# Decode layer on one core: VectorE's instructions for two groups as a loop of seven turns, with semaphores counted down

## The chip, the cores and the metric

One core of one Trainium2 chip runs the whole kernel. The metric is the device time of one execution in microseconds; the kernel before has a median of 1291.82 us in three runs (1291.61 to 1292.01).

## The reference

One decode step of a transformer layer, batch 4, one query position, model width 512: layer norm, attention with 32 heads of 128 over a cache of 8192 positions for each head, output projection, residual, a second layer norm, a gated feed-forward block of width 1792, residual. All tensors are bfloat16.

```python
q = (layernorm(x) @ wq).reshape(B, 1, 32, 128).transpose(0, 2, 1, 3)
scores = einsum("bhqd,bhkd->bhqk", q, k_cache) * 128 ** -0.5
o = einsum("bhqk,bhkd->bhqd", softmax(scores), v_cache)
h = x + o.transpose(0, 2, 1, 3).reshape(B, 1, 4096) @ wo
n = layernorm(h)
out = h + (sigmoid(n @ w_gate) * (n @ w_up)) @ w_down
```

The two caches have 268 MB each; the weights add about 14 MB.

## The kernel before

**Pairs and groups.** The 128 (batch, head) combinations are taken two at a time: 64 pairs (`NP`), each with 4 MB of K and 4 MB of V. Four pairs (`GP`) make a group, and a group's softmax is done at once; there are 16 groups. The steps (L365) are K of pairs 0 to 3, and then K of pair n + 4 and V of pair n in turn (`LAGP` is 4). Each step has eight chunks (`NCH`).

**Transfers.** SyncE (SP) issues every large load in the order of the list of steps, into the four slots of `KV` (L327 to L335). A slot is taken again when its last user is done: `freed` (L312) gives the token of the last `scores` of a K pair or of the last `pv` of a V pair, and SP's queue waits for it ahead of the DMA. The feed-forward weights use the same slots at the end; `w_down` comes in three pieces (`WDT`, L342). K of pair 0 and V of pair 63 come in four pieces each. `wo` is loaded over `wq` once the q projection (`t_qproj`) has been computed (L360).

**A K step.** For each chunk VectorE transposes 128x1024 words out of `KV` into one of four buffers `kTc` (`transposes`, L410 to L413), and TensorE multiplies them with the masked query windows `Lq` (`scores`, L430). VectorE fills the four `Lq` buffers ahead (`q_windows`, L574 to L578). After a group's fourth pair `softmax` (L441) takes maximum, exponential, sum and division through VectorE, TensorE and ScalarE, in four parts p1 to p4 that are due 1, 3, 6 and 8 chunks later; p4 writes the probabilities, transposed, into `PT` (L484).

**A V step.** `pv` (L487) multiplies `PT` with V on TensorE. After a group's last pair, `finish` (L514) evicts the sum with ScalarE, collects rows (L523) and, for each second group, makes `O_row` and `OT` on VectorE (L528, L530), projects with `wo` (L540) and adds to `sth` (L545).

**Order and semaphores.** `_Prog` collects a list of instructions for each engine. `emit` (L76) works out which semaphores an instruction has to wait for, and `_wait` (L70) puts the wait ahead of it. VectorE and ScalarE have two semaphores each: one for what TensorE waits for (`dve>pe`, `act>pe`), one for all others. TensorE has one, `pe`, that only goes up. What TensorE waits for is counted down again by the waiter (`sem_inc(..., -v)`, L74), so that each wait is for the same number in each turn of a loop.

**The loop.** TensorE's list is cut (L592 to L599) ahead of K of pairs 8, 16, ..., 56 and of V of pair 60. The seven stretches between are equal and are run as one body in `Fori`, seven turns (L698 to L710). The lists of the other engines, VectorE's among them (L692), are written out in full.

**After the loop** come the last four V steps, the residual and second layer norm (`layernorm`, L238), the feed-forward block (L635 to L642), `f_res` (L651), the three parts of `f_down` (L659 to L663), the eviction to `o_sb` (L668) and the store (L669).

Of the kernel before, what the change touches and what calls it, by code (L numbers as in the profile page):

```python
# [5 lines left out]
BF16 = mybir.dt.bfloat16  # L6
# [5 lines left out]
NSL = 4  # L12
NKT = 4
# [7 lines left out]
class _Prog:  # L21
# [6 lines left out]

    ENGS = ("sp", "act", "dve", "pool", "pe")
    SPLIT = ("dve", "act")  # L30
# [14 lines left out]
    def _as_seen(self, eng, t):  # L45
        key, v = t
        if key not in self.SPLIT:
            return t
        want = (eng == "pe")
        for to_pe, n in self.kind[key][v - 1:]:  # L50
            if to_pe == want:
                return (key + ">pe" if want else key + ">", n)
# [23 lines left out]
    def emit(self, eng, fn, waits=(), incs=1, to_pe=False, sig=None):  # L76
# [4 lines left out]
        if eng in self.SPLIT and incs:  # L81
            assert incs == 1
# [14 lines left out]
        if eng == "pe":  # L97
            run.same = (sig, tuple(todo), incs)
        return tok

    def dma(self, eng, key, fn, waits=()):
# [8 lines left out]
        return tok  # L110


def bass_sequential_preLN__mha_block_cached__glu_gated_glu__decode_kernel(
# [32 lines left out]
    with ExitStack() as es:  # L146
# [19 lines left out]
        q2 = SB("q2", [128, 4, NH], BF16)  # L166
# [45 lines left out]
        keys = ["sp", "act>", "act>pe", "dve>", "dve>pe", "pool", "pe", "x", "out", "wg", "wu", "wd0", "wd1", "wd2", "wq", "wo"]  # L212
        prog.own = {f"vs{i}" for i in range(NSL)}
# [24 lines left out]
        def layernorm(st, t_st, i, dst, mbank, t_bank):  # L238
            w = lnw[:, i, :]
            n = NDC * B  # L240
            t1 = emit("dve", lambda e: e.tensor_tensor(st[:, n:2 * n], st[:, 0:n], st[:, 0:n], ALU.mult), [t_st])

            tr = emit("dve", lambda e: e.tensor_reduce(
                lnr[:, i, :], st[:, :].rearrange("p (k c) -> p k c", c=NDC), AX.X, ALU.add), [t1], to_pe=True)
            t2 = emit("pe", lambda e: e.matmul(mbank[:, 0:2 * B], onesf[:, :], lnr[:, i, :], start=True, stop=True),
                      [tr, t_ones, t_bank])
            t3 = emit("dve", lambda e: e.tensor_copy(w[:, 0:2 * B], mbank[:, 0:2 * B]), [t2])
            t4 = emit("dve", lambda e: e.tensor_tensor(w[:, 8:8 + B], w[:, 0:B], w[:, 0:B], ALU.mult), [t3])
            t5 = emit("dve", lambda e: e.scalar_tensor_tensor(
                out=w[:, 12:12 + B], in0=w[:, B:2 * B], scalar=EPS, in1=w[:, 8:8 + B],  # L250
                op0=ALU.add, op1=ALU.subtract), [t4])
            ts = emit("act", lambda e: e.activation(w[:, 20:20 + B], w[:, 12:12 + B], ACT.Sqrt), [t5])
# [4 lines left out]
                cen, st[:, 0:n].rearrange("p (b c) -> p b c", b=B), mean, ALU.subtract), [t3])  # L257
            t6 = emit("dve", lambda e: e.reciprocal(w[:, 16:16 + B], w[:, 20:20 + B]), [ts])
            return emit("dve", lambda e: e.tensor_tensor(
                dst[:, :].rearrange("p (b c) -> p b c", b=B), cen, rstd, ALU.mult), [t6, t7], to_pe=True), t3  # L260
# [11 lines left out]
        t_xT = emit("pe", f_xT, [t_x, t_ident])  # L272
# [14 lines left out]
        for hh in range(2):  # L287
# [4 lines left out]
            amask[:, :], identf[:, :].rearrange("p (a j) -> p a j", a=4), AX.X, ALU.max), [t_identf])  # L292
# [8 lines left out]
        t_pv = {}  # L301
        t_wq = []
# [9 lines left out]
        def freed(job):  # L312
# [3 lines left out]
            t = t_score.get(NCH * n + NCH - 1) if kind == "k" else t_pv.get(n)  # L316
# [93 lines left out]
        def transposes(n, s):  # L410
# [3 lines left out]
                kTc[:, u % NKT, :], chunk(n, slot, s)), [t_k[n][s * len(t_k[n]) // NCH], t_score.get(u - NKT)], to_pe=True)  # L414
# [24 lines left out]
        turn = {}  # L439

        def softmax(g):  # L441

            t_mx = emit("dve", lambda e: e.tensor_reduce(mpart[:, :], sbank(g), AX.X, ALU.max),  # L443
                        [t_score[GP * NCH * (g + 1) - 1], st_.get("p1")], to_pe=True)
            box = {}

            def p1():
                box["p1"] = emit("pe", lambda e: e.matmul(  # L448
                    bank[XS][0:1, 0:128], mpart[:, 0:1], identf[:, :], start=True, stop=True),
                    [t_mx, t_identf, st_["xs"]], sig="p1")  # L450
# [4 lines left out]
                    [box["p1"]])  # L455
                box["d2"] = emit("dve", lambda e: e.tensor_copy(
                    rowpad[0:1, :].rearrange("p (z k i) -> p z k i", z=2, i=GP),
                    bass.AP(raw(mrow), 0, [[GH, 1], [GP, 2], [0, 16], [1, GP]])), [d2, t_rp0], to_pe=True)

            def p2():  # L460
                t = emit("pe", lambda e: e.matmul(  # L461
                    bank[XS][:, 128:129], rowpad[:, :], identf[:, 0:1], start=True, stop=True),
                    [box["d2"], t_rp0], sig="p2")
                a1 = emit("dve", lambda e: e.tensor_scalar(  # L464
                    negmb[:, :], bank[XS][:, 128:129], -SCALE, None, op0=ALU.mult), [t])
                box["a2"] = emit("act", lambda e: e.activation(  # L466
                    E_sb[:, :], sbank(g), ACT.Exp, bias=negmb[:, 0:1], scale=SCALE, accum_out=sig[:, 0:1]),
                    [a1], to_pe=True)
                st_["exp"] = t_exp[g] = box["a2"]

            def p3():
                t = emit("pe", lambda e: e.matmul(  # L472
                    bank[XS][:, 130:131], Gmat[:, :], sig[:, 0:1], start=True, stop=True), [box["a2"], t_gm], sig="p3")
                d3 = st_["xs"] = emit("dve", lambda e: e.reciprocal(rsum[:, :], bank[XS][:, 130:131]), [t])  # L474
                box["d4"] = emit("dve", lambda e: e.tensor_scalar(
                    E_sb[:, :], E_sb[:, :], rsum[:, 0:1], None, op0=ALU.mult), [d3])

            def p4():
                pb = g % 2
                w = [box["d4"], t_pt0, t_pvg.get(g - 2)]  # L480
                for z in range(2):
                    dst = bass.AP(raw(PT), 64 * z * 2 * PTW + pb * PTW + 4 * z,
                                  [[2 * PTW, 64], [128, 2 * RC], [1, 4], [40, GP]])
                    t_ptc[g] = emit("dve", lambda e, z=z, dst=dst: e.transpose(dst, E_sb[64 * z:64 * z + 64, :]), w, to_pe=z == 1)  # L484
            return [(1, p1), (3, p2), (6, p3), (8, p4)]

        def pv(u):  # L487
# [20 lines left out]
            tok = emit("pe", f, w, incs=4 if last else 1, sig=("pv", slot, g % 2, i, m, n == 0, first, last))  # L508
# [5 lines left out]
        def finish(g):  # L514
            t_oev[g] = emit("act", lambda e: e.activation(O_sb[:, :], obank(g), ACT.Copy),  # L515
                            [t_pvg[g], st_.get("sel")], to_pe=True)
            lo = 64 * (g % 2)

            def s1():
# [6 lines left out]
                st_["sel"] = emit("pe", f, [t_oev[g], t_pk, st_["xo"]], sig=("collect", lo))  # L526
                if g % 2:
                    t = emit("dve", lambda e: e.tensor_copy(O_row[:, :], bank[XO][:, 0:128]),  # L528
                             [st_["sel"], st_.get("tr")])
                    st_["tr"] = emit("dve", lambda e: e.transpose(  # L530
                        OT[:, :, :], O_row[:, :].rearrange("p (i e) -> p e i", e=4)), [t, st_.get("ot")], to_pe=True)
                    st_["xo"] = t

            def s2():
                def f(e):
                    ins = None
                    for c in range(NDC):
                        for k in range(4):
                            at = (4 * turn.get("g", g // 2) + k) * D + 128 * c
# [4 lines left out]
                st_["ot"] = t = emit("pe", f, [st_["tr"], st_["xo"]], sig="project")  # L544
                st_["h"] = st_["xo"] = emit("dve", lambda e: e.tensor_tensor(  # L545
                    sth[:, 0:NDC * B], sth[:, 0:NDC * B], bank[XO][:, 128:128 + NDC * B], ALU.add), [t, st_["h"]])
            return [(2, s1), (4, s2)] if g % 2 else [(2, s1)]

        def q_projection():
# [8 lines left out]
            t = emit("pe", f, [t_wq[0], t_xn, t_xTc, t_h])  # L558
            t_qproj.append(t)
            tq = emit("dve", lambda e: e.tensor_copy(q_all[:, :], bank[XO][:, 0:NH]), [t], to_pe=True)  # L560

            def f2(e):
                ins = None
                for ce in range(4):
                    ins = e.matmul(bank[XO][:, NH * ce:NH * (ce + 1)], selrep[:, ce, :], q_all[:, :],
                                   start=True, stop=True)
                return ins
            t2 = emit("pe", f2, [tq, t_sr])
            st_["q"] = st_["xo"] = emit("dve", lambda e: e.tensor_copy(
                q2[:, :, :].rearrange("p e n -> p (e n)"), bank[XO][:, 0:4 * NH]), [t2])  # L570
# [3 lines left out]
        def q_windows(n):  # L574
            dst = bass.AP(raw(Lq), n % NLQ * 4 * W + 31, [[NLQ * 4 * W, 128], [W, 4], [64, 2], [32, 2]])
            src = bass.AP(raw(q2), GH * (n % NP // GP) + n % GP, [[4 * NH, 128], [NH, 4], [GP, 2], [0, 2]])
            keep = bass.AP(raw(amask), 0, [[4, 128], [0, 4], [2, 2], [1, 2]])
            t_lq[n] = emit("dve", lambda e: e.tensor_tensor(dst, src, keep, ALU.mult),  # L578
                           [st_["q"], t_lq0, t_am, t_score.get(NCH * (n - NLQ + 1) - 1)], to_pe=True)
# [13 lines left out]
        for kind, n in steps:  # L593
            if kind == "k" and n and n % (2 * GP) == 0:
                if not cuts:
                    emit("pe", lambda e: [], t_wo, incs=0)
                cuts.append(len(prog.ops["pe"]))
            if (kind, n) == ("v", NP - LAGP):
                cuts.append(len(prog.ops["pe"]))  # L599
            for m in range(NCH):  # L600
                u = NCH * n + m
                if kind == "k":
# [13 lines left out]
        while chain:  # L616
# [6 lines left out]
        emit("act", lambda e: e.activation(dummy[:, 0:1], sig[:, 0:1], ACT.Sqrt), [st_["xs"]])  # L623
        t_res = emit("dve", lambda e: e.tensor_copy(
            res[:, :, 0:25:8], sth[:, 0:NDC * B].rearrange("p (b c) -> p c b", b=B)), [st_["h"], t_rs0], to_pe=True)
# [4 lines left out]
        def glu_mm(wv, bk):  # L630
# [8 lines left out]
        t_g = emit("pe", glu_mm(t_w["wg"][0], bank[XO]), [t_hn, t_w["wg"][1], st_["xo"]])  # L639
        t_sg = emit("act", lambda e: e.activation(sg_sb[:, :], bank[XO][:, 0:NF], ACT.Sigmoid), [t_g])  # L640
        t_u = emit("pe", glu_mm(t_w["wu"][0], bank[UBK]), [t_hn, t_w["wu"][1]])
        t_hh = emit("dve", lambda e: e.tensor_tensor(  # L642
            hhT[:, :, 0:25:8], sg_sb[:, :].rearrange("p (t b) -> p t b", b=B),
            bank[UBK][:, 0:NF].rearrange("p (t b) -> p t b", b=B), ALU.mult), [t_sg, t_u, t_hh0], to_pe=True)
# [12 lines left out]
        t_r = emit("pe", f_res, [t_res])  # L657
        for i in range(len(WDT) - 1):
# [8 lines left out]
            t_d = emit("pe", f_down, [t_hh, t_wd[i], t_r], incs=4)  # L667
        t_oc = emit("dve", lambda e: e.tensor_copy(o_sb[:, :], bank[DBK][:, 0:128]), [t_d])  # L668
# [6 lines left out]
        with nc.Block() as block:  # L675
# [16 lines left out]
            def _(dve):  # L692
                for fn in prog.ops["dve"]:
                    fn(dve)

            @block.tensor
            def _(pe):
                ops = prog.ops["pe"]  # L698
                body = ops[cuts[0]:cuts[1]]
                for a, b in zip(cuts[1:], cuts[2:]):  # L700
                    assert [x.same for x in ops[a:b]] == [x.same for x in body]
                for fn in ops[:cuts[0]]:
                    fn(pe)
                with pe.Fori(0, len(cuts) - 1) as i:
                    turn["g"] = i
                    for fn in body:
                        fn(pe)
                    del turn["g"]
# [30 lines left out]
```

## Time and profile before

| what | before |
|---|---|
| median of three runs | 1291.82 us |
| the profiled execution, its own time | 1291.74 us |
| span in its profile, first to last instruction | 1290.0 us |
| bytes read from HBM | 550.77 MB, 427 GB/s over the span |
| TensorE matmul busy | 781.4 us (61%) |
| VectorE busy | 723.8 us (56%), 765 instructions |
| ScalarE, GpSimd busy | 28.0 us, 10.9 us |
| granted TensorE clock, mean | 0.792 |

The times in a page count from the first instruction. A group of instructions is a line with its engine, operation, tiles and number, then busy time and the mean of one, then the engine's idle time ahead of them with what ended it. "PEq L74" as the releaser is TensorE's own queue at the countdown of line 74.

Besides the instructions the trace keeps DMA packets, with queue, start and size, and the events by which a transfer counts its semaphore up: sixteen for each of the large loads, one by each DMA engine. Which engine an event belongs to isn't recorded. The table gives, for some loads, the time of the first of the sixteen events, and by how much the last and the second last of the sixteen came after it.

| load, first event at (us) | last event later by | second last later by |
|---|---|---|
| 17.48 | 0.38 | 0.38 |
| 42.40 | 1.53 | 0.37 |
| 52.13 | 1.52 | 1.23 |
| 236.68 | 1.94 | 1.92 |
| 246.39 | 2.22 | 1.94 |
| 294.96 | 2.24 | 1.93 |
| 314.38 | 3.06 | 2.25 |
| 460.10 | 3.04 | 2.25 |
| 469.82 | 3.24 | 3.04 |
| 683.52 | 3.27 | 3.03 |
| 703.07 | 4.12 | 2.91 |
| 897.36 | 4.13 | 2.88 |
| 916.80 | 5.11 | 2.88 |
| 1120.78 | 5.13 | 2.86 |
| 1140.20 | 6.10 | 2.87 |
| 1247.06 | 6.13 | 2.86 |
| 1256.76 | 6.20 | 3.28 |
| 1282.02 (last piece of `w_down`) | 4.89 | 2.02 |

Packets of the kind "instruction" are in two queues. Queue 8 has twelve of 16,384 bytes, at 18.3, 65.3, 103.9, 127.0, 165.9, 203.7, 235.4, 258.3, 305.7, 1256.8, 1282.5 and 1286.6 us. Queue 14 has packets of 8,192 bytes, seven of them inside the span, at 44.65, 243.53, 463.11, 691.18, 696.40, 905.88 and 1130.29 us. TensorE's branch instructions, which end a turn of its loop, stand at 302.0, 458.5, 613.4, 769.8, 926.5, 1082.7 and 1238.1 us.

### The profile page before, as it was taken

The page shows a single profiled execution, that of the slowest core. Times are in us where ns is not written, and L with a number is a line of the kernel's source. Part 1 is how long each engine was busy: PE and PEld are TensorE (multiplying, and loading weights), DVE is VectorE, ACT ScalarE, POOL GpSimd, SP SyncE. Part 2 cuts the span into 40 slices and gives each one's busy share as a digit, 9 for nine tenths or more (in the row PEclk, how much of TensorE's full clock was granted, in tenths as well). Part 3 has the DMA queues.
Part 4 walks back from the last instruction along what each step waited for, and adds up shares of the span by engine and source line. Part 5 has one row for each costly group of instructions (what it writes and reads, how often), then busy time and mean ns, then how long its engine had stood idle before and what let it go on. Part 6 is the DMA issues. An engine that isn't in the chain of part 4 may idle for free. (4 is left out here: it accounts for less than half of the span.)

```text
span 1290.0 us, 11331 instructions
## 1 busy us (share of the span) xinstructions
PE 781.4 (61%) x4768; PEld 315.5 (24%) x4768; DVE 723.8 (56%) x765; ACT 28.0 (2%) x56; POOL 10.9 (1%) x13
## 2 busy tenths in 40 slices
PE   4566656647557556566556666476465666566464
PEld 2222212213213222222212222132122222222122
DVE  5594745737555555556637556465545647457340
ACT  0000000000000000000000000000000000000001
POOL 3000000000000000000000000000000000000000
PEclk9698778778788687687788887787787886777775
DMA  9999999999999999999999999999999999999997
GB/s 396 432 430 430 434 427 436 424 434 427 436 429 434 431 431 433 429 436 427 436 430 433 432 430 432 430 437 426 437 427 435 433 429 436 426 437 428 435 424 299
DMA packets 23423, 551.04 MB, mean 427 GB/s; under 512 B 2280, under 2 KB 4076, under 8 KB 6124
## 3 DMA queue, kind: packets, MB, share of 16 engines
q1 hardware_dynamic: 23396, 550.78, 99.6%
q8 instruction: 12, 0.20, 0.1%
q14 instruction: 7, 0.06, 0.0%
q10 hardware_dynamic: 8, 0.00, 0.0%
HBM read 550.77 MB, written 0.00 MB: 427 GB/s over the span
## 5 line engine op out<-in xcount | busy, mean ns | idle before, releaser
L430 PE MATMUL PS<-kTc,Lq 128*128 128x512 bf16 x2048 | 587.2, 445 | 440.0 <-PEq L74 435.6
L413 DVE STREAM_TRANSPOSE kTc<-KV 128x1024 f32<-128x1024 f32 x512 | 587.0, 1209 | 346.4 <-DMA KV<-in_A_k_cache_dram 340.6
L430 PEld LDWEIGHTS PS<-kTc,Lq 128*128 128x128 bf16 x2048 | 211.8, 109 | 803.2 <-issue 662.4
L505 PE MATMUL PS<-KV,PT 128*32 128x512 bf16 x2048 | 135.8, 397 | 23.4 <-PEq L74 18.9
L484 DVE STREAM_TRANSPOSE PT<-E_sb 64x512 bf16<-64x512 bf16 x32 | 78.4, 2450 | 1.0
L578 DVE TENSOR_TENSOR Lq<-q,amask 128x16 bf16<-128x16 bf16 x68 | 15.1, 229 | 98.7 <-PE PS L430 98.7
L505 PEld LDWEIGHTS PS<-KV,PT 128*32 128x32 bf16 x2048 | 48.7, 99 | 85.9 <-issue 46.3
L466 ACT ACTIVATE E_sb<-PS,negmb 128x512 bf16<-128x512 f32 x16 | 11.0, 687 | 1191.2 <-DVE negmb L464 1191.2
L523 PE MATMUL PS<-O_sb,pick 128*64 128x128 f32 x128 | 31.5, 428 | 0.9 <-PEq L74 0.9
L528 DVE CAST O_row<-PS 128x128 bf16<-128x128 f32 x8 | 2.3, 291 | 52.8 <-PE PS L523 52.8
L523 PEld LDWEIGHTS PS<-O_sb,pick 128*64 128x64 f32 x128 | 25.1, 224 | 13.9 <-issue 13.9
L448 PE MATMUL PS<-identf,mpart 128*1 128x128 f32 x32 | 6.1, 270 | 15.4 <-PEq L74 15.4
L474 DVE RECIPROCAL rsum<-PS 128x1 f32<-128x1 f32 x16 | 2.7, 169 | 20.4 <-PE PS L472 20.4
L540 PE MATMUL PS<-OT,Wreg 128*128 128x4 bf16 x128 | 10.6, 172 | 0.8 <-PEq L74 0.8
L443 DVE TENSOR_REDUCE mpart<-PS 128x1 f32<-128x512 f32 x16 | 10.9, 684 | 0.0
L618 POOL MEMSET kTc<- 128x448 bf16 x1 | 0.5, 471 | 1223.2 <-PE PS L430 1223.2
L515 ACT ACTIVATE O_sb<-PS 128x512 f32<-128x512 f32 x16 | 9.6, 597 | 55.3 <-PE PS L505 55.3
L540 PEld LDWEIGHTS PS<-OT,Wreg 128*128 (+1 forms) x128 | 8.7, 97 | 4.8 <-issue 1.2
L452 DVE TENSOR_REDUCE mrow<-PS 1x8 f32<-1x128 f32 x16 | 4.4, 276 | 8.4 <-PE PS L448 8.4
L472 PE MATMUL PS<-sig,Gmat 128*128 128x1 f32 x32 | 5.6, 244 | 5.9 <-PEq L74 5.9
L554 PE MATMUL PS<-xnT,Wreg 128*128 128x4 bf16 x128 | 3.6, 166 | 8.9 <-PEq L74 8.9
L461 PE MATMUL PS<-identf,rowpad 128*128 128x1 f32 x32 | 5.6, 244 | 4.2 <-PEq L74 4.2
(70 smaller groups left out, 77.4 us busy)
## 6 DMA issues: line engine op xcount, KB each, us to landing
KV<-in_A_k_cache_dram SPq DMA_DIRECT2D x63, 4096.0 KB, 28.1
KV<-in_A_v_cache_dram SPq DMA_DIRECT2D x63, 4096.0 KB, 34.9
Wreg<-in_A_wq_dram SPq DMA_DIRECT2D x1, 4096.0 KB, 12.2
KV<-in_A_k_cache_dram SPq DMA_DIRECT2D x4, 1024.0 KB, 17.8
Wreg<-in_A_wo_dram SPq DMA_DIRECT2D x1, 4096.0 KB, 27.3
KV<-in_A_v_cache_dram SPq DMA_DIRECT2D x4, 1024.0 KB, 29.4
KV<-in_B_w_gate_dram SPq DMA_DIRECT2D x1, 1792.0 KB, 28.1
KV<-in_B_w_up_dram SPq DMA_DIRECT2D x1, 1792.0 KB, 25.0
```

The source lines that it names most:

```text
L413: t_copy[u] = emit("dve", lambda e: e.transpose(kTc[:, u % NKT, :], chunk(n, slot, s)), [t_k[n][s * len(t_k[n]) // NCH], t_score.get(u - N ...
L430: ins = e.matmul(sbank(g), Lq[:, n % NLQ, ce, off:off + 128], k3[:, :, ce // 2, :, ce % 2], start=first and ce == 0, stop=last and ce == 3)
L443: t_mx = emit("dve", lambda e: e.tensor_reduce(mpart[:, :], sbank(g), AX.X, ALU.max), [t_score[GP * NCH * (g + 1) - 1], st_.get("p1")], to ...
L448: box["p1"] = emit("pe", lambda e: e.matmul(bank[XS][0:1, 0:128], mpart[:, 0:1], identf[:, :], start=True, stop=True), [t_mx, t_identf, st ...
L461: t = emit("pe", lambda e: e.matmul(bank[XS][:, 128:129], rowpad[:, :], identf[:, 0:1], start=True, stop=True), [box["d2"], t_rp0], sig="p2")
L466: box["a2"] = emit("act", lambda e: e.activation(E_sb[:, :], sbank(g), ACT.Exp, bias=negmb[:, 0:1], scale=SCALE, accum_out=sig[:, 0:1]), [ ...
L484: t_ptc[g] = emit("dve", lambda e, z=z, dst=dst: e.transpose(dst, E_sb[64 * z:64 * z + 64, :]), w, to_pe=z == 1)
L505: mms.append(e.matmul(obank(g)[32 * j:32 * (j + 1), :], PT[:, g % 2, o:o + 32], in_slot(slot, *at), start=first, stop=last, tile_position= ...
L515: t_oev[g] = emit("act", lambda e: e.activation(O_sb[:, :], obank(g), ACT.Copy), [t_pvg[g], st_.get("sel")], to_pe=True)
L523: ins = e.matmul(bank[XO][lo:lo + 64, 0:128], pick[:, q, :], O_sb[:, 128 * q:128 * (q + 1)], start=(q == 0), stop=(q == 3), tile_position= ...
L540: ins = e.matmul(cols(bank[XO][:, 128:128 + NDC * B], c), Wreg[:, bass.ds(at, 128)], OT[:, k, 0:B], start=(k == 0), stop=(k == 3))
L578: t_lq[n] = emit("dve", lambda e: e.tensor_tensor(dst, src, keep, ALU.mult), [st_["q"], t_lq0, t_am, t_score.get(NCH * (n - NLQ + 1) - 1)] ...
```

## The change

VectorE's list is cut at the same seven places as TensorE's and run as a loop of seven turns by the new function `looped`, which now serves both engines. For that, what VectorE waits for is counted down too, on semaphores of its own (`pe>dve`, `act>dve`, `dve>dve`, and those of the K slots, `sl0` to `sl3`), and each instruction says by `to=` which engine it tells. An instruction tells one engine, so what SP, ScalarE and GpSimd wait for of TensorE comes from instructions with `to=""`. Several things follow:

- The `scores` tell VectorE. The slot of K of pair n (n from 4 on) is therefore given back by the first `pv` chunk of pair n - 4 (`t_pv0`), the next such instruction on TensorE; for K of pairs 0 to 3 VectorE does a small memset after the last scores (`t_kf`).
- `q_windows` takes its source at an offset that holds the turn's number, and `q2` is wider by `GH` zero columns.
- The second half of the q projection is four instructions with a token each; the load of `wo` waits for the first of them.
- The waits for tokens of the same engine are dropped on TensorE (`f_down` for `f_res`) and ScalarE's eviction of `obank` no longer waits for `st_["sel"]`. The early `Sqrt` of the tail reads `identf` instead of `sig`.

```diff
-    SPLIT = ("dve", "act")
+    SPLIT = ("pe", "dve", "act")
+    LOOPED = ("pe", "dve")
+    TELLS = {"pe": "dve", "dve": "dve"}
...
-            less = key.endswith(">pe") or key in self.own
+            less = key.endswith((">pe", ">dve")) or key in self.own
...
-    def emit(self, eng, fn, waits=(), incs=1, to_pe=False, sig=None):
+    def emit(self, eng, fn, waits=(), incs=1, to=None, sig=None):
+
+        to = self.TELLS.get(eng, "") if to is None else to
...
-            key = eng + (">pe" if to_pe else ">")
-            self.total[key] = self.total.get(key, 0) + 1
-            self.kind[eng].append((to_pe, self.total[key]))
+            key = f"{eng}>{to}"
+            n = self.total.get(key, 0)
+            self.total[key] = n + incs
+            self.kind[eng] += [(to, n + 1 + i) for i in range(incs)]
...
+    def looped(self, eng, e, cuts, turn):
+        ops = self.ops[eng]
+        cuts = [c[eng] for c in cuts]
+        body = ops[cuts[0]:cuts[1]]
+        for a, b in zip(cuts[1:], cuts[2:]):
+            assert [x.same for x in ops[a:b]] == [x.same for x in body]
+        assert all(x.same[0] for x in body)
+        for fn in ops[:cuts[0]]:
+            fn(e)
+        with e.Fori(0, len(cuts) - 1) as i:
+            turn["i"] = i
+            for fn in body:
+                fn(e)
+            del turn["i"]
+        for fn in ops[cuts[-1]:]:
+            fn(e)
...
-        prog.own = {f"vs{i}" for i in range(NSL)}
+        prog.own = {f"{c}{i}" for c in ("sl", "vs") for i in range(NSL)}
...
-            t = t_score.get(NCH * n + NCH - 1) if kind == "k" else t_pv.get(n)
+            t = t_pv.get(n) if kind == "v" else t_kf.get(n) if n < LAGP else t_pv0.get(n - LAGP)
...
-                kTc[:, u % NKT, :], chunk(n, slot, s)), [t_k[n][s * len(t_k[n]) // NCH], t_score.get(u - NKT)], to_pe=True)
+                kTc[:, u % NKT, :], chunk(n, slot, s)), [t_k[n][s * len(t_k[n]) // NCH], t_score.get(u - NKT)], to="pe", sig=("transpose", u % NKT, slot, s, n == 0))
...
+            if m == 0:
+                t_pv0[n] = tok
...
-                            [t_pvg[g], st_.get("sel")], to_pe=True)
+                            [t_pvg[g]], to="pe")
...
+            for ce in range(4):
+                t2 = emit("pe", lambda e, ce=ce: f2(e, ce), [tq, t_sr], to="dve" if ce else "")
+                if ce == 0:
+                    t_qproj.append(t2)
+            tz = emit("dve", lambda e: e.memset(q2[:, :, NH:], 0.0), to="dve")
...
+            def f(e):
+                at = GH * (n // GP) + n % GP
+                if "i" in turn_d:
+                    at = 2 * GH * turn_d["i"] + at
+                src = q2[:, :, bass.ds(at, GP + 1)][:, :, 0:GP + 1:GP]
+                src = bass.AP(src.tensor, src.offset, [list(src.ap[0]), list(src.ap[1]), list(src.ap[2]), [0, 2]])
+                return e.tensor_tensor(dst, src, keep, ALU.mult)
...
+                        if n < LAGP:
+                            t_kf[n] = emit("dve", lambda e: e.memset(dummy[:, 1:2], 0.0), [t_score[u]], to="")
...
-            t_d = emit("pe", f_down, [t_hh, t_wd[i], t_r], incs=4)
+            t_d = emit("pe", f_down, [t_hh, t_wd[i]], incs=4, to="dve")
...
-                for fn in prog.ops["dve"]:
-                    fn(dve)
+                prog.looped("dve", dve, cuts, turn_d)
```

The shared instructions of the softmax, of `finish` and of `layernorm` get a `to=` and a `sig=` each, and are otherwise as they were.

More of the change, by code (lines that the diff above doesn't have):

```diff
@@ L48, in _as_seen @@
             return t
[L49 to L52, printed above, removed]
+        want = eng if eng in self.LOOPED else ""
+        for to, n in self.kind[key][v - 1:]:
+            if to == want:
+                return (f"{key}>{to}", n)
         raise AssertionError(f"{eng} waits for {t}, and nothing later tells it")
@@ L96, in emit @@
         self.ops[eng].append(run)
-        if eng == "pe":
-            run.same = (sig, tuple(todo), incs)
+        run.same = (sig, tuple(todo), incs, key)
         return tok
@@ L291, in bass_sequential_preLN__mha_block_cached__glu_gated_glu__decode_kernel @@
         t_am = emit("dve", lambda e: e.tensor_reduce(
-            amask[:, :], identf[:, :].rearrange("p (a j) -> p a j", a=4), AX.X, ALU.max), [t_identf])
+            amask[:, :], identf[:, :].rearrange("p (a j) -> p a j", a=4), AX.X, ALU.max), [t_identf], to="dve")
         for c in range(2):
@@ L301, in bass_sequential_preLN__mha_block_cached__glu_gated_glu__decode_kernel @@
         t_pv = {}
+        t_pv0 = {}
+        t_kf = {}
         t_wq = []
@@ L507, in f @@
                 return mms if last else mms[-1]
-            tok = emit("pe", f, w, incs=4 if last else 1, sig=("pv", slot, g % 2, i, m, n == 0, first, last))
+            tok = emit("pe", f, w, incs=4 if last else 1, to="", sig=("pv", slot, g % 2, i, m, n == 0, first, last))
+            if m == 0:
+                t_pv0[n] = tok
             if m == NCH - 1:
@@ L538, in f @@
                         for k in range(4):
-                            at = (4 * turn.get("g", g // 2) + k) * D + 128 * c
+                            at = (4 * turn.get("i", g // 2) + k) * D + 128 * c
                             ins = e.matmul(cols(bank[XO][:, 128:128 + NDC * B], c),
@@ L656, in f_res @@
             return ins
-        t_r = emit("pe", f_res, [t_res])
+        emit("pe", f_res, [t_res])
         for i in range(len(WDT) - 1):
@@ L692, in _ @@
             def _(dve):
-                for fn in prog.ops["dve"]:
-                    fn(dve)
+                prog.looped("dve", dve, cuts, turn_d)
             @block.tensor
             def _(pe):
[L698 to L708, printed above, removed]
-                for fn in ops[cuts[-1]:]:
-                    fn(pe)
+                prog.looped("pe", pe, cuts, turn)
 _INS = ['A_x', 'A_k_cache', 'A_v_cache', 'A_wq', 'A_wo', 'B_x', 'B_w_gate', 'B_w_up', 'B_w_down']
```

101 lines of the change are left out of this document (48 added, 53 removed).

## The prediction

> **What bounds the kernel now.** First the page's head, busy times and DMA queues (packets, MB, share of sixteen engines' span):
>
> ```profile
> span 1290.0 us, 11331 instructions
> PE 781.4 (61%) x4768; PEld 315.5 (24%) x4768; DVE 723.8 (56%) x765; ACT 28.0 (2%) x56; POOL 10.9 (1%) x13
> ...
> DMA  9999999999999999999999999999999999999997
> ...
> q1 hardware_dynamic: 23396, 550.78, 99.6%
> q8 instruction: 12, 0.20, 0.1%
> q14 instruction: 7, 0.06, 0.0%
> ```
>
> The loads fill the DMA engines from start to end, and VectorE, which the change rewrites, idles 44% of the span. Then the end of the chain of waits (start, us, what):
>
> ```profile
> 1269.76 8.64 SPq L342
> 1278.40 0.04 issue
> 1278.44 8.47 DMA KV<-in_B_w_down_dram
> 1286.91 0.04 issue
> 1286.96 0.51 PE PS L663 x8
> ```
>
> The end is the last piece of `w_down` plus eight matmuls, an eviction and the store. So the question is what makes that piece land at 1286.91. The sixteen completion events of each load answer it: the first engine reports the piece at 1282.02, the last at 1286.91, the second last 2.87 us before that. One engine is late alone. Its lag grows in steps of about 1 us, and the steps fall on queue 14's 8 KB packets: 1.26 to 2.22 around 243.53 (from the middle of the sixteen to last), 2.25 to 3.24 around 463.11 (from second last to last), 3.27 to 4.12 around 691.18, 4.13 to 5.11 around 905.88, 5.13 to 6.10 around 1130.29. The first, at 44.65, raised an engine from 0.36 to 1.23. At these six packets VectorE has 48, 176, 303, 434, 559 and 689 recorded instructions behind it: one packet for each 128, so 64 bytes an instruction, and some 80 unrecorded ones at the front. They are VectorE's program being fetched, all through one DMA engine (my reading: the events carry no engine's name). TensorE's fetches, on queue 8, rise different engines in turn, and its loop does without. The DMA view of 306.5 to 1250 us shows it:
>
> ```profile
> q1 hardware_dynamic: 13980, 407.25, 100.3%
> q14 instruction: 5, 0.04, 0.0%
> ```
>
> No line of queue 8 is there, though TensorE jumps back five times in that window. All five packets but one (696.40, where SP passes its own boundary) are VectorE's.
>
> **The change part by part.**
>
> *VectorE's program.* Removed are the written-out copies. I count the new list by the code: ahead of the loop 80 unrecorded, 119 compute instructions (27 of the head, 64 transposes, 8 windows, 4 memsets, 16 of two softmaxes) and about 73 waits; body 64 transposes + 8 windows + 16 + 3 = 91 (the windows of the trace show 91 in each turn), 6 waits for each of 8 pairs + 6 for each of 2 groups + 3 = 63, and some 10 for the loop and the windows' offsets (TensorE's records have one such for each offset slice); tail about 40. That is 272 + 164 + 40 = 476 instead of 80 + 776 = 856, so boundaries at 128, 256 and 384 are passed, three fetches instead of six; a fourth needs 512, 36 more than I count. The three that go took 0.85 + 0.98 + 0.97 = 2.8 us of that engine's lead over the first. What is late next: the engine at 3.28 after TensorE's fetch at 1256.76, which stays. That leaves a gain of 2.87, the gap of the last piece, since the late engine would then stand at about 6.2 - 2.9 = 3.3 too. I take -2.87; bounds -1.9 (a fourth fetch) and -3.0 (the largest gap among the tail's rows, 2.97).
>
> A loop needs its body kept on the engine. Mine spans instructions 272 to 436, two blocks of 128 (10 KB). TensorE's body has 1211 records, 78 KB or five to six of its 16 KB blocks, and six turns of it bring no packet. No row shows how much VectorE keeps; the nearest row says far more than two blocks, so I take 0 for refetching; the other bound is a rival.
>
> [...]
>
> *About 500 waits become instructions of their own.* Before, VectorE's waits ride on its instructions; TensorE's countdowns are separate records (651). Price, from the tail, below: the product into `hhT`, which has a separate wait ahead of it, starts 0.10 us after L635's end (1284.24 to 1284.34); the addition L545, which has none, 0.05 after L540's. On TensorE, a weight load follows VectorE's L456 by 0.12 us, and ScalarE's exponential, without a countdown, follows L464 by 0.03. So 0.05 to 0.09 each, 0.07 taken: 500 x 0.07 = 35 us of engine time in all. In the loop it lies beside 340.6 us in which the transposes wait for K's DMA: 6 x 0.07 = 0.4 us for each pair, where a K step's idle is several us. Cost 0; without that cover 0.4 us for each of 64 pairs, 27 us.
>
> *K slots given back later.* The rows of a softmax step (start, us, engine):
>
> ```profile
> 609.70 0.33 SPq L335 DMA_DIRECT2D KV<-in_A_k_cache_dram  x1
> 609.71 0.23 DVE L578 TENSOR_TENSOR Lq<-q,amask 128x16 bf16<-128x16 bf16 x1 [1.22 <-PE PS L430]
> ...
> 610.78 0.66 PE L505 MATMUL PS<-KV,PT 128*32 128x512 bf16 x8
> ```
>
> SP issues K at the last scores (609.70); behind the first `pv` chunk it would be about 611.1, 1.4 us later (0.5 in a plain step). Behind it in SP's queue is the next V. K lands 28.1 us after its issue, of which its own transfer takes 9.7 (the pitch of the landings), so 18.4 us of other loads lie ahead of it and the wait costs 0; uncovered it would be up to 1.4 us for each of 60 loads. It could gain nothing, since the engines are full. The `wo` load comes 0.6 us later (L565 ends at 17.64, not L554 at 16.6), behind K of pair 1, which lands at 33.7: 0. The memsets `t_kf` follow a `q_windows` that waits for the same scores, and VectorE's next transposes wait for K anyway: 0. SP, ScalarE, GpSimd wait for the same work under other names.
>
> *The tail.*
>
> ```profile
> 1281.11 3.13 PE L635 MATMUL PS<-hnT,KV 128*128 128x4 bf16 x112 [1.41 <-PEq L74]
> ...
> 1284.34 0.40 DVE L642 TENSOR_TENSOR kTc<-sg_sb,PS 128x56 bf16<-128x56 f32 x1 [3.38 <-PE PS L635]
> 1285.02 0.81 PEld L663 LDWEIGHTS PS<-KV,kTc 128*32 128x32 bf16 x32 [0.65 <-DMA KV<-in_B_w_down_dram]
> ```
>
> `hhT` is ready at 1284.74, the first piece of `w_down` at 1284.79. From V's last landing to `hhT` I count nine more waits on VectorE (L528, L530, L545, two and then five of `layernorm`): 9 x 0.07 = 0.63 us. The 56 matmuls take 56 x 0.0325 (1.04 us for 32) = 1.82, so they would end up to 0.25 us later than now, less the dropped wait for `f_res` (0.2). I take +0.1, bounds 0 and +0.3. The wait ahead of L668 is on the path: +0.07. All these landings come 2.87 earlier together, V's last pieces too, so the tail's own order holds.
>
> **Sum.** The profiled span 1290.0 - 2.87 + 0.10 + 0.07 = 1287.3; its own time is 1.74 longer, 1289.04. The median of the runs lies 0.08 above the profiled time: **1289.1 us**, 0.21% less. Bounds: 1291.82 - 3.0 = 1288.8 and 1291.82 - 1.9 + 0.37 = 1290.3; with 0.4 for prices read off single rows 1288.4 to 1290.7.
>
> **Rivals.**
>
> (1) *The loop is refetched.* If VectorE kept too little, each of six jumps back would bring one or two packets, all on the late engine, which after three fetches stands at 3.3. One each: 3.3 + 6 x 0.98 = 9.2 against 6.2, **1294.9**, slower; two each: 15.0, **1300.8**. It decides from three refetches on, where today's six are reached again. For it: packets are half as large as TensorE's, so VectorE may keep less. Against: TensorE's five blocks.
>
> (2) *A fourth fetch* (my count short by 36), or the tail's waits cost their upper price: 1291.82 - 1.9 + 0.3 = **1290.2**, no change. For it: the unrecorded instructions are only inferred.
>
> (3) *It doesn't shorten what it should:* packets move to another engine that is late, or the wait for the ring that held `w_down`'s issue for 8.64 us sets the end: **1291.9**. Against: the issue ended at 1278.40, 0.9 after the late engine finished `w_gate` (1277.51), so it moves with that engine.
>
> (4) *Late K slots run the queue dry.* Needs 18 us; no row has it. Left out of the chances.
>
> **Chances.** Forecast 0.66, one refetch a turn 0.10, two 0.09, (2) 0.10, (3) 0.05. A measurement of this kernel can tell about 0.2%, 2.6 us, from no change: the border is 1289.24. Of the forecast's 0.66 I put 0.52 below it and 0.14 above. Faster 0.52; same 0.14 + 0.10 + 0.05 = 0.29; slower 0.19. Predicted 1289.1. The range for eight in ten: 1288.3 to 1295.4, which takes in all but the two refetches a turn (0.09) and the edges; the forecast's own is 1288.4 to 1290.7.
>
> **What would show it.** Right: queue 14 has three packets of VectorE's and SP's one inside the span, none of VectorE's between about 310 and 1230; the last event of the K loads stays about 3.3 us behind the first to the end; last and second last differ by under 0.5 in the tail; the page's list has VectorE's semaphore rows, transposes still x512. The pitch of the landings stays at 9.71. Wrong: more packets on queue 14 in step with the turns and a lag that grows by 1 us with each; or a lag of 4 at the end (a fourth fetch); or a DMA row with zeros before 1280 (slots too late); or, with the lag at 3.3, an end no earlier, which would put the tail's VectorE chain on the path.

## The result and the profile after

The changed kernel takes 1284.57 us in the median of six runs (1284.42 to 1284.97); the kernel before took 1291.76 beside it. The ratio is 0.9945, with a 95% interval of 0.9932 to 0.9957: 7.2 us faster, where 2.7 were forecast. The profiled execution's own time is 1284.61, its span 1282.8.

The page of the changed kernel: head, busy times, DMA queues (packets, MB, share of sixteen engines' span), and VectorE's two groups with most idle time ahead of them (busy, mean ns | idle, its releaser).

```profile
span 1282.8 us, 11908 instructions
PE 770.9 (60%) x4768; PEld 309.8 (24%) x4768; DVE 723.7 (56%) x770; ACT 28.0 (2%) x56; POOL 11.0 (1%) x13
...
q1 hardware_dynamic: 23396, 550.78, 99.7%
q8 instruction: 11, 0.18, 0.0%
q14 instruction: 4, 0.03, 0.0%
...
L437 DVE STREAM_TRANSPOSE kTc<-KV 128x1024 f32<-128x1024 f32 x512 | 587.6, 1210 | 317.0 <-DVEq L78 316.5
...
L612 DVE TENSOR_TENSOR Lq<-q,amask 128x16 bf16<-128x16 bf16 x68 | 15.2, 230 | 107.5 <-DVEq L78 107.3
```

The same two groups in the kernel before:

```profile
L413 DVE STREAM_TRANSPOSE kTc<-KV 128x1024 f32<-128x1024 f32 x512 | 587.0, 1209 | 346.4 <-DMA KV<-in_A_k_cache_dram 340.6
...
L578 DVE TENSOR_TENSOR Lq<-q,amask 128x16 bf16<-128x16 bf16 x68 | 15.1, 229 | 98.7 <-PE PS L430 98.7
```

The DMA engines are as full as before (99.7% in queue 1 for 99.6) and VectorE is as busy (723.7 us for 723.8). Its waits now end at its own queue's countdown (`DVEq L78`) and no longer at a load or at TensorE: the separate wait instructions are there, 577 more instructions in the head. The idle time ahead of the two groups hasn't grown: it is 424.5 us together, for 445.1 before. Queue 14 has three packets fewer. The DMA view of the loop, 306.5 to 1230 us:

```profile
q1 hardware_dynamic: 13729, 400.07, 100.3%
q14 instruction: 1, 0.01, 0.0%
```

The one packet left, at 695.13, is SP's by the count: SP has 79 recorded instructions behind it there, as at 696.40 before. Five jumps back of VectorE's loop lie in this window (458, 613, 769, 923 and 1079 us) and bring nothing. Then the chain of waits (start, us, what), which is all there is of it:

```profile
1280.29 0.08 issue
1280.37 0.29 DVE o_sb L705
```

Before, this chain led back to the last piece of `w_down`. Now it breaks off ahead of the eviction, because the wait of that eviction is a separate instruction; what lies behind it has to be read from the timeline of the tail.

The events by which the loads count up, in both kernels:

| | before | after |
|---|---|---|
| time from load to load in the loop, first engine | 9.715 us | 9.683 us |
| mean time of a 32 KB packet, 310 to 1230 us | 1217.0 ns | 1213.0 ns |
| last engine behind the first, a K or V load near 1250 us | 6.1 to 6.2 us | 2.9 us |
| first engine's event of V's last piece | 1266.73 | 1262.17 |
| last piece of `w_down`, last engine | 1286.91 | 1278.76 |

So two things changed in the loads: the late engine has lost 3.2 us of its lag (2.9 were forecast), and the first engine is 4.6 us earlier too, at a pace that is 0.33% quicker from the first load into `KV` on. Nothing in the forecast makes that.

### The profile page after: what moved, and what is told of

It is laid out like the page before. It is cut to its first block, busy times and chain, and to the rows that moved or that the text cites. A ratio compares the mean times of both kernels' runs of the same rounds, so it can differ in the third digit from the quotient of the medians.

```text
span 1282.8 us, 11908 instructions
## 1 busy us (share of the span) xinstructions
PE 770.9 (60%) x4768; PEld 309.8 (24%) x4768; DVE 723.7 (56%) x770; ACT 28.0 (2%) x56; POOL 11.0 (1%) x13
## 3 DMA queue, kind: packets, MB, share of 16 engines
q1 hardware_dynamic: 23396, 550.78, 99.7%
## 5 line engine op out<-in xcount | busy, mean ns | idle before, releaser
L454 PE MATMUL PS<-kTc,Lq 128*128 128x512 bf16 x2048 | 577.8, 436 | 435.3 <-PEq L78 426.9
L454 PEld LDWEIGHTS PS<-kTc,Lq 128*128 128x128 bf16 x2048 | 206.1, 107 | 794.7 <-issue 654.4
```

The lines of the kernel that those rows point to most:

```text
L454: ins = e.matmul(sbank(g), Lq[:, n % NLQ, ce, off:off + 128], k3[:, :, ce // 2, :, ce % 2], start=first and ce == 0, stop=last and ce == 3)
```

## The experiments

Of the pace there were three theories. A: the wider `q2` moves what is laid out behind it by 64 bytes, `KV` from byte 27328 of each partition to 27392, and the place of `KV` sets the time of a packet. B: the K slots given back later. C: VectorE's work, spaced by its new waits, disturbs the loads less.

**e1, the kernel before with a gap of 64 bytes**

```diff
+        SB("gap", [128, 32], BF16)
         Lq = SB("Lq", [128, NLQ, 4, W], BF16)
```

> The kernel before with 64 unused bytes in each partition behind q2, which put KV, kTc and PT where the changed kernel has them (KV from byte 27328, 64 beyond a multiple of 128, to 27392, a multiple of 128). The list of VectorE is as before. Theory A (the place of KV sets the time of a 32 KB packet: 1217 ns on the mean before, 1213 after): packets of 1213 ns, loads every 9.68 us instead of 9.72, six fetches of VectorE and a last engine that still ends 6 us behind; 1291.8 - 4.2 = about 1287.5. Theory B (packets are shorter because K's slots are given back later): 1291.8. Theory C (because VectorE's work is spaced by its new waits): 1291.8.

Measured: 1285.91 us, ratio 0.9955 (0.9938 to 0.9971). Packets of 1213.2 ns, loads every 9.682 us, the last engine 5.7 us behind. An unused tensor of 64 bytes gives 5.9 of the 7.2 us, with VectorE's list, semaphores and slots as before. It gives more than the 4.2 that theory A put on the pitch: 131 loads x 0.033 = 4.3, and the packets of the small rows at the end are shorter too (1 KB rows of `w_down` 46.7 ns for 51.2, 3.5 KB rows 140 for 144.3; 1792 and 1024 of them on 16 engines make 0.5 and 0.3 us). These make 5.1; the last engine's lag at the last piece, 4.6 us for 4.9, is 0.3 more.

**e2, the changed kernel with q2 behind KV**

```diff
-        q2 = SB("q2", [128, 4, NH + GH], BF16)
         Lq = SB("Lq", [128, NLQ, 4, W], BF16)
         KV = SB("KV", [128, NSL, R * 128], BF16)
+        q2 = SB("q2", [128, 4, NH + GH], BF16)
```

> The changed kernel with q2 laid out behind KV: KV begins at byte 26304, again 64 beyond a multiple of 128; kTc, PT and Wreg stay where the change has them. Theory A: packets of 1217 ns and loads every 9.72 us, with three fetches and a last engine 3 us behind; about 1284.6 + 4.2 = 1288.8, which is near the forecast of 1289.1. Theories B and C: 1284.6.

Measured: 1289.61 us, ratio 0.9984 (0.9974 to 0.9993). Packets of 1216.9 ns, loads every 9.715 us, the last engine 3.3 us behind. This is the change without the new place of `KV`, and nearly what the forecast was about. The last piece of `w_down` lands at 1284.04, 2.87 us earlier than before, which is the forecast's term. That it agrees to the hundredth is luck, since the runs of e2 alone differ by 0.4 us. The time falls by 2.16 only, and the tail's timeline shows where the rest went (start, us, engine, instruction, idle ahead):

```profile
1282.47 0.41 DVE L679 TENSOR_TENSOR kTc<-sg_sb,PS 128x56 bf16<-128x56 f32 x1 [3.42 <-DVEq L78]
1282.99 0.91 PEld L700 LDWEIGHTS PS<-KV,kTc 128*32 128x32 bf16 x34 [0.54 <-issue]
1283.03 1.12 PE L700 MATMUL PS<-KV,kTc 128*32 128x128 bf16 x33
1284.48 0.83 PE L700 MATMUL PS<-KV,kTc 128*32 128x128 bf16 x23 [0.34 <-issue]
...
1285.50 0.29 DVE L705 CAST o_sb<-PS 128x128 bf16<-128x128 f32 x1 [2.62 <-DVEq L78]
```

The product into `hhT` is ready at 1282.88, a microsecond after the first piece of `w_down` (1281.91); the matmuls start only then, stop once for 0.34 us, and the eviction starts 1.46 us after the last landing instead of 0.58.

**e3, the kernel before with late K slots**

```diff
-            t = t_score.get(NCH * n + NCH - 1) if kind == "k" else t_pv.get(n)
+            t = t_pv.get(n) if kind == "v" else t_score.get(NCH * n + NCH - 1) if n < LAGP else t_pv0.get(n - LAGP)
...
+            if m == 0:
+                t_pv0[n] = tok
```

> The kernel before, with K's slots (from pair 4 on) given back by the first pv chunk of pair n - 4, as the change does, and nothing else. Theory A: no change, 1291.8, packets of 1217 ns. Theory B: packets of 1213 ns, 1287.5. Theory C: 1291.8.

Measured: 1291.72 us, ratio 1.000 (0.9991 to 1.001); packets of 1217.1 ns. The later slots cost and gain nothing. Theory B falls. C falls with e2, whose VectorE runs just as in the changed kernel at the old pace.

**e4, the changed kernel with VectorE's list written out**

```diff
-                prog.looped("dve", dve, cuts, turn_d)
+                for fn in prog.ops["dve"]:
+                    fn(dve)
```

> The changed kernel with VectorE's list written out in full, its counted-down waits kept: about 80 + 1340 instructions, so some ten fetches on queue 14 instead of three. If each puts one DMA engine back by 0.98 us, that engine ends 3.1 + 7 x 0.98 = 10 us behind the first instead of 2.9, and the time is 1284.6 + 6.9 = about 1291.5, at packets of 1213 ns. If the fetches don't set the end: 1284.6.

Measured: 1290.10 us, ratio 0.9987 (0.9977 to 0.9996). The DMA view of the same window, 306.5 to 1230:

```profile
q1 hardware_dynamic: 13722, 399.87, 100.3%
q14 instruction: 8, 0.07, 0.0%
```

Seven of these eight are VectorE's; with three ahead of the window it fetches ten times. The last engine's lag climbs by 0.7 to 0.9 us with each, to 8.9 us, where 0.98 each and 10 in all were expected. At the last piece it is 4.2. My reading is that the fast engines had run out of work there, because SP's issue of `w_down` waited for the late one: it ends at 1277.71, 2.5 us after the late engine's event of `w_gate`; in the kernel before it ends 2.3 after that event. So the time is 1.4 below the expected 1291.5. With three, six and ten fetches (changed kernel, e1, e4, all at the quick pace) the lag is 2.9, 5.7 and 8.9 and the time 1284.57, 1285.91 and 1290.10. Of the three, e4 differs from the changed kernel in the loop alone: with the same counted-down waits the loop is worth 5.5 us. The step from three to six is small in the time because e1 has the old tail, and other things, below, end the changed kernel.

Next, which place of `KV` is quick. In e6, e7 and e8 small tensors are moved from ahead of `KV` to behind it in the kernel before; `kTc`, `PT` and `Wreg` stay where they were.

**e6, lnr behind KV**

> The kernel before with the 64 bytes of lnr laid out behind KV instead of ahead of it: KV begins at byte 27264, a multiple of 128 and 128 beyond a multiple of 256; kTc, PT and Wreg stay. Theory P (a packet is only short when KV begins at a multiple of 256): packets of 1217 ns, 1291.8. Theory Q (a multiple of 128 is enough): packets of 1213 ns, 1285.9. Theory R (the place of kTc, PT or Wreg is what counts, not that of KV): 1291.8.

**e7, stx and lnr behind KV**

> The kernel before with stx and lnr (192 bytes) laid out behind KV: KV begins at byte 27136, a multiple of 512; kTc, PT and Wreg stay. Theories P and Q: packets of 1213 ns, loads every 9.68 us, 1285.9. Theory R: packets of 1217 ns, 1291.8.

**e8, M8 behind KV**

> The kernel before with the 32 bytes of M8 laid out behind KV: KV begins at byte 27296, 32 beyond a multiple of 128 (160 beyond one of 256). Theory P: packets as long as in the kernel before, 1217 ns, 1291.8. Theory Q: the same, 1291.8. If the cost grows with how far KV is off (from 64 to 32 bytes): longer packets and a time above 1292.5.

```diff
-        lnr = SB("lnr", [128, 2, 2 * B], FP32)
...
         KV = SB("KV", [128, NSL, R * 128], BF16)
+        lnr = SB("lnr", [128, 2, 2 * B], FP32)
```

(e6; e7 moves `stx` as well, e8 `M8` alone.) Measured, with the other kernels beside them:

| kernel | KV begins at | beyond a multiple of 256 | 32 KB packet, mean | load to load | median | ratio, interval |
|---|---|---|---|---|---|---|
| before | 27328 | 192 | 1217.0 ns | 9.715 us | 1291.8 us | |
| e2 | 26304 | 192 | 1216.9 | 9.715 | 1289.61 | 0.9984 (0.9974 to 0.9993) |
| e8 | 27296 | 160 | 1217.2 | 9.713 | 1291.37 | 0.9997 (0.9988 to 1.0006) |
| e6 | 27264 | 128 | 1217.3 | 9.713 | 1291.02 | 0.9995 (0.9986 to 1.0005) |
| e1 | 27392 | 0 | 1213.2 | 9.682 | 1285.91 | 0.9955 (0.9938 to 0.9971) |
| e7 | 27136 | 0 | 1213.2 | 9.681 | 1285.87 | 0.9955 (0.9939 to 0.9971) |
| after | 27392 | 0 | 1213.0 | 9.683 | 1284.57 | 0.9945 (0.9932 to 0.9957) |

Theory P holds: a start at a multiple of 256 is quick, 128 isn't enough, and 128, 160 and 192 beyond cost the same (less than 128 beyond wasn't tried). The differences between these places follow from the sizes of the tensors; that the quick ones are multiples of 256 rests on where the allocator starts, which no trace shows. It isn't `kTc`, `PT` or `Wreg`, since e7 leaves them where they were and e2 leaves them where the change put them.

`Lq` lies 5120 bytes (20 x 256) ahead of `KV` in all seven kernels, so it shares its place. But the loads differ while it isn't in use: the first piece of K, ahead of the first write of a window into `Lq` at 18.41 us, comes 2.48 to 2.50 us after the load ahead of it in the slow kernels and 2.43 in the quick ones; and at the end, after the last use of `Lq`, the small rows are slow as well. Nor does it take an engine that works beside the loads: in the kernel before TensorE, VectorE, ScalarE and GpSimd all stand still from 1257 to 1263 us, and 90% of the 8 KB packets there take more than 309 ns (0.4% in the changed kernel).

No run shows why a start at the other places costs time. What the packets show is how much: 1217.0 ns for 1213.0 on the mean, 0.33%.

Last, the tail. In the changed kernel its timeline reads:

```profile
1272.82 0.17 DVE L269 COPY lnw<-PS 128x8 f32<-128x8 f32 x1 [0.86 <-DVEq L78]
1273.13 0.16 DVE L270 TENSOR_TENSOR lnw<-lnw 128x4 f32<-128x4 f32 x1
...
1277.91 0.40 DVE L679 TENSOR_TENSOR kTc<-sg_sb,PS 128x56 bf16<-128x56 f32 x1 [3.43 <-DVEq L78]
1278.43 1.45 PEld L700 LDWEIGHTS PS<-KV,kTc 128*32 128x32 bf16 x56 [0.54 <-issue]
1278.46 1.68 PE L700 MATMUL PS<-KV,kTc 128*32 128x128 bf16 x56
1280.37 0.29 DVE L705 CAST o_sb<-PS 128x128 bf16<-128x128 f32 x1 [2.05 <-DVEq L78]
```

From the end of L269 (1272.99) to L270 are 0.14 us. In the kernel before, the same pair (1279.91 to 1279.94) had 0.03:

```profile
1279.74 0.17 DVE L247 COPY lnw<-PS 128x8 f32<-128x8 f32 x1 [0.75 <-PE PS L245]
1279.94 0.16 DVE L248 TENSOR_TENSOR lnw<-lnw 128x4 f32<-128x4 f32 x1
```

So a counted-down wait cost 0.11 us between these two small dependent instructions (0.14 for 0.03). From V's last landing to the product into `hhT` the changed kernel takes 12.9 us, the kernel before 11.8. All 56 matmuls then run in one go: two pieces of `w_down` were there, the third landed meanwhile, and VectorE's chain ends last.

**e5, no countdown after the loop**

```diff
-            todo.append((key, v - self.known[eng].get(key, 0) if less else v, less))
+            todo.append((key, v - self.base[eng].get(key, 0) if less else v, less and not self.tail))
+            if less and not self.tail:
+                self.base[eng][key] = v
             self.known[eng][key] = v
...
+                prog.tail = True
```

> The changed kernel, in which VectorE and TensorE after the loop wait for the running count (a wait that rides on the instruction) and count nothing down. Theory A (the counted-down waits cost about 0.11 us each on the chain from V's last piece to the feed-forward product, and made that chain the last to end): VectorE's small copies of the second layer norm follow each other after 0.03 us again instead of 0.14, the product is ready about 11.7 us after V's last landing instead of 12.9, the last piece of w_down (landing at 1278.76) sets the end again, and the time is 1.0 us less, 1283.5. Theory B (the tail is late because of the landings alone): 1284.6.

Measured: 1284.57 us, ratio 0.9945 (0.9931 to 0.9959): no faster than the changed kernel, as theory B had it. The mechanism of theory A is there all the same: L273 and L274 (1271.90 to 1271.93) are 0.03 us apart again, and the product is ready 11.5 us after V's last landing, and the next rows show what took its place:

```profile
1276.26 0.40 DVE L684 TENSOR_TENSOR kTc<-sg_sb,PS 128x56 bf16<-128x56 f32 x1 [3.31 <-PE PS L677]
...
1276.71 1.04 PE L705 MATMUL PS<-KV,kTc 128*32 128x128 bf16 x32
1277.97 0.13 PEld L705 LDWEIGHTS PS<-KV,kTc 128*32 128x32 bf16 x5 [0.48 <-DMA KV<-in_B_w_down_dram]
1277.97 0.40 PE L705 MATMUL PS<-KV,kTc 128*32 128x128 bf16 x5 [0.21 <-DMA KV<-in_B_w_down_dram]
...
1279.01 0.72 PE L705 MATMUL PS<-KV,kTc 128*32 128x128 bf16 x19 [0.65 <-issue]
```

TensorE stands still for 0.65 us after 37 of 56 matmuls, waiting for nothing that the profile shows. A packet of queue 8 begins at 1276.77 in this run, and TensorE goes on 2.24 us after that. I take the packets of this queue for fetches of TensorE's own program: in the kernel before, the nine up to 305.68 us come 260 recorded instructions of TensorE apart on the mean.

**e9 and e10, the fetch moved**

e9 is e5 with these matmuls behind the loop; e10 is the changed kernel with them.

```diff
+                def f_pad(e):
+                    for _ in range(60):
+                        e.matmul(bank[DBK][:, 0:4], ident[:, :], ident[:, 0:4], start=True, stop=True)
+                    return []
+                emit("pe", f_pad, incs=0)
```

> The run e5 (no countdown after the loop) with 60 unused matmuls on TensorE behind the loop, at a point where it waits for V; they make its program 120 instructions longer there and shift where the program's fetches on queue 8 fall. In e5 TensorE stood still for 0.65 us in the middle of the last matmuls, after a fetch that began at 1276.77. Theory A (TensorE waited there for its own instructions): the fetch falls before 1272, the gap is gone, the end follows the last landing by 0.6 us again, and the time is 0.5 to 0.7 us below e5's, about 1283.9. Theory B (the gap has another cause, and the tail is bound by something else): 1284.5, with the gap still there.

> The changed kernel with the same 60 unused matmuls behind the loop and its counted-down waits kept in the tail. Theory A: the chain through VectorE is ready at about 1278.3 and sets the end, as in the changed kernel; moving the fetch gains nothing, 1284.5. If the fetch alone had set the end of the changed kernel: 1283.9.

Measured for e9: 1283.54 us, ratio 0.9938 (0.9924 to 0.9951), 1.0 us below the changed kernel and the best of this study. One fetch now falls at 1266.46 (another still begins at 1276.89), the gap is gone, and the chain of waits leads back to the load as in the kernel before:

```profile
1262.22 8.38 SPq L370
1270.60 0.04 issue
1270.64 7.99 DMA KV<-in_B_w_down_dram
1278.63 0.04 issue
1278.68 0.51 PE PS L711 x8
1279.19 0.02 issue
1279.21 0.29 DVE o_sb L716
```

Measured for e10: 1285.68 us in the median, ratio 0.9951 (0.9936 to 0.9967), with runs of 1284.66, 1284.80, 1286.57 and 1286.83. Both expectations missed, though the two short runs lie where theory A put them. The profiled run is one of the longer two, and its timeline shows the same wait at a worse place:

```profile
1274.40 2.64 PE L678 MATMUL PS<-hnT,KV 128*128 128x4 bf16 x94 [1.96 <-PEq L78]
...
1279.09 0.64 PE L678 MATMUL PS<-hnT,KV 128*128 128x4 bf16 x18 [2.04 <-issue]
```

TensorE loses 2.04 us in the feed-forward matmuls, ahead of VectorE's product, with a fetch that begins at 1276.83 and the next matmul 2.26 us after that. In both kernels the fetch ahead of it begins at 1241.4; in e9 the next one had begun at 1266.46. A late fetch doesn't stop TensorE by itself: the changed kernel has one at 1276.79, e9 the one at 1276.89, and neither stops in its last matmuls. That the instructions of this fetch are what TensorE waits for fits these times, but the profile doesn't name it.

What makes a fetch begin early or late, and why only half of e10's runs are long, isn't settled. The place in the program alone doesn't do it: in the changed kernel, e5, e9 and e10 a fetch begins at 1276.77 to 1276.89, with 192, 102, 94 and 170 recorded instructions of TensorE still to come. In all four that is 1.1 to 1.5 us after the first DMA engine's event of the last load. That e9 is shorter than e5 is measured; that it stays so where the program is moved by a few instructions isn't.

## Why the prediction was wrong, point by point

**The bound: right.** The loads fill the DMA engines (99.7% of the span), one engine was late alone before, by 6.1 to 6.2 us near the end, and VectorE's fetches made it late. Three packets of VectorE's are left, as counted, and none in the loop; the body has 162 records (164 counted), and the list from start to end, with one turn, has some 446 instructions (476 counted: the first fetch falls at 64 recorded instructions, not at 48); the lag near the end is 2.9 us (about 3.3 forecast). e4 shows the same from the other side.

**The rivals: fell,** but for half of one. No refetch: six jumps back, no packet. That is shown for a body of 162 records, 1.3 times the 128 to 129 instructions that lie between VectorE's packets (at 64, 193 and 321 recorded ones); how long a body VectorE's loop could have without a refetch no run shows. No fourth fetch; no lag of another engine grew in its place (2.9 us for the last, near 1250 us). What holds the issue of `w_down` no view names; it ends 2.5 us after the late engine's event of `w_gate` in the changed kernel too. The second half of (2) did come: the tail cost more than its upper price.

**The step that failed** is one the sum doesn't have. I wrote "The pitch of the landings stays at 9.71", and let each part of the change act through instructions, waits and slots. That `q2` is wider by `GH` columns stood in my account of the change as a matter of its contents; that it moves `KV` by 64 bytes, to a multiple of 256, was nowhere. That alone gives 5.9 us (e1, and e7 by another way), more than the rest of the change. The direction was forecast; the larger part of the size is luck of the layout. With `KV` at its old offset the change takes 1289.61 (e2), inside the forecast's own range of 1288.4 to 1290.7.

**The tail: mis-sized.** I took 0.07 us for a counted-down wait, which the runs put at 0.11, and +0.17 for the tail; in e2 it is +0.88 (1.46 instead of 0.58 from the last landing to the eviction). Nine waits at 0.11 are 1.0 us of the 1.2 by which the way from V's last landing to the product has grown. The sentence that "the tail's own order holds" fell: VectorE's chain came to end last. I hadn't looked at where the packets of queue 8 fall in the tail; TensorE's next stops stand behind one of them, 0.65 us in e5 and 2.04 in e10.

**K slots, the waits in the loop: right** at nothing (e3 for the slots; VectorE's idle time in the page for the waits). The later `wo` and the memsets weren't tried alone; e2, which has them, leaves no room for a large price.

The 7.2 us, then, are 5.0 from the place of `KV` (e2 to the changed kernel) and 2.2 from the loop and its waits (before to e2); in the other order 5.9 (e1) and 1.3. The loop's share differs because the tail takes back part of what the landings gain: 2.87 us earlier with 2.16 left in e2, 2.45 earlier (1281.21 in e1 to 1278.76) with 1.34 left at the quick pace.

## What to carry to other kernels

Where loads bound a kernel, compare the time of one packet (here 1217.0 ns for 1213.0) before comparing engines, and list each tensor whose size an edit changes: what is laid out behind it moves, as `KV` did by 64 bytes. A start of the loads' target at a multiple of 256 bytes was worth 0.45% here (e1), at the cost of 64 unused bytes. And an average over sixteen DMA engines hides the one that is late (99.6% before, with the last engine 6.1 us behind the first): the spread of a load's completion events shows it.

## What the runs showed of the hardware that I hadn't expected

- From 310 to 1230 us a packet of 32 KB took 1213 ns, nearly without exception, in the changed kernel with its `KV` at a multiple of 256, and mostly 1214 to 1225 in the kernel before; 1 KB rows at the end took 46.0 ns on the mean against 51.2.
- The cost is there from the first load into `KV`, but a packet's own time doesn't show it at once: in the kernel before, the 8 KB packets of K's first pair take 309 ns up to 18 us, as after the change, and from 20 us on many take 312 to 319. The landings of the same pieces are apart already, 2.50 and 2.49 us for 2.43 and 2.44. So go by the spacing of the landings.
- `Wreg` begins 96 beyond a multiple of 256 (160 after the change). The 4 KB packets of `wo`, which go there, take mostly 159 ns at first; from 40 to 42 us their median is 164, in both kernels. In the changed kernel the loads into `KV` are quick but for a few beside these packets. No run puts `Wreg` at a multiple of 256, so whether that would gain anything is open.
- With a fetch of 8 KB, whose packet takes 0.31 to 0.34 us, the lag of one engine (my reading: the events carry no engine's name) grew by 0.7 to 1.0 us, and it stayed while the queue was full: in the kernel before 6.10 us at 1140.20 and 6.13 at 1247.06.
- TensorE stood still for 0.34, 0.65 and 2.04 us in dense runs of short matmuls (e2, e5, e10), and each time went on 2.2 to 2.6 us after a fetch on queue 8 had begun, while the DMA engines were loaded; with an earlier fetch (e9) it didn't stop there.
